# A windowed-attention and feed-forward kernel on one core: later exponentials kept as fp32 in PSUM, turns at PSUM banks in the work list, small key copies moved, list constants changed

## The chip, the cores and the metric

The kernel runs on one core of a Trainium2 chip. Its time is the device time of one execution in microseconds; lower is better. The core has TensorE (PE, matrix products), VectorE (DVE), ScalarE (ACT), GpSimd (POOL) and SyncE (SP), each with its own queue of instructions, which it works off in order; they wait for each other by semaphores. Sixteen DMA engines move data between HBM and the on-chip SBUF. Products land in PSUM, which has eight banks.

## The reference

Attention over 8 batches, 8 heads, 576 positions and head size 64, then a two-layer feed-forward part:

```
scores = q @ k^T / 8
heads 0-3: keep 0 <= i - j < 32
heads 4-7: keep 0 <= i - j < 128 and (i - j) % 4 == 0
attn = softmax over the kept scores;  x = attn @ v       (4608 x 512 after joining heads)
h = x @ w_in (512 x 2048);  g = max(0.01 h, h);  out = g @ w_out (2048 x 512)
```

All inputs and the output are fp32; the kernel works on fp16 operands.

## The kernel before, in words

**A list, planned and then issued.** The kernel first builds a list of tasks (`plan.add`). Each has the engines that may do it, an assumed duration for each, a delay until its result may be used, and the tasks it depends on. `_Plan.forward` plays the list through: it gives each task an engine and a start. `backward` turns that into priorities, and `run` repeats both nine times and keeps the best order. Then every engine's instructions are issued in the order of planned starts. So the order on every queue is fixed when the kernel is built, out of assumed durations; on the chip an instruction that finds its input late holds up everything behind it on its engine. `MARGIN` stretches the assumed durations after `CALM` microseconds; `LATE` and `RAMP` are additional delays assumed for the landing of loads. `FIRST` is the order of the loads of the first two batches and of the weights ("r" the last 64 positions of q and k, "q", "v" with batch and head group, "w" a 512 KB piece of the weights, "." a place for the second part of an earlier "v" load, "c" the mask tables).

`share` goes over the finished order and makes a cast of POOL wait for the VectorE task of kind "m" before it, where the two would run together.

**Attention.** One visit (`attend`, `turn`, `unit`) handles two heads of a batch, one on partitions 0-63 and one on 64-127. Queries and keys are loaded, cast to fp16 (`cast`, L387 on DVE and POOL, L386 on ACT), transposed and copied into slots (`move`, L400 on DVE and POOL, L398 on ACT). For the batches 0 and 1 TensorE transposes (L654, L697) into the PSUM bank `tp` (and, in batch 0, two more banks), and the copies read that bank. For the batches from 2 on VectorE transposes blocks of 32 (L619, L624, L631) in SBUF; in the dilated visits each half of the keys is then copied in two pieces, 64x512 and the last 64x64.

A visit has two units. In each, TensorE makes the scores of a narrow band of keys and queries into a bank `p_bank` (L775, tagged "s"), ScalarE takes the exponential (L782) and VectorE multiplies it with a table of zeros and ones (L786, tagged "m"). Batches 0 and 1 need no such mask, since TensorE adds a bias of -60000 there (`by_pe`, L771). A product with ones gives the sums, into the same `p_bank` (L793, or L810 where VectorE or POOL first added overlapping columns, L802), and a product with the values goes to a second bank (L793). ScalarE takes the logarithm (L818) of the sums and the exponential of its negative (L820), and VectorE multiplies this into the values' product (L831), which gives a piece of xt. The three banks sps, ops0 and ops1 go around for this (with hps and fps in the first batches); `ee` has four buffers for the exponentials.

**Feed-forward.** Twelve chunks of 384 rows. "Up" products of xt with w_in go to the banks hps (L850; L879 for the second chunk, in two halves), ScalarE applies the leaky activation into gt (L865, L891). "Down" products with w_out are plain for the first four 128-row tiles (L916, copied out at L924). The other tiles go in groups of four with seven half-size products in place of eight (L1006), for which VectorE forms sums of gt (L992) and of w_out (L946) and ScalarE and VectorE collect the results (L1035, L1037, L1043). The last three chunks do their "up" products in the same way (L1201, L1226, L1275, L1287, L1289, L1295, L1302). Attention of later batches and the feed-forward part of earlier ones run interleaved, so that between a unit's scores and its sums TensorE has other products to do.

The mask is these lines:

```
t_e = add("ACT", 0.06 + n * 0.00085, 0.22, [t_s] + e_old, ... activation(out=et, in_=p_bank, Exp))
t_m = t_e if by_pe else add("DVE", 0.45, 0.15, [t_e, t_con[0]],
        ... tensor_tensor(out=et, in0=et, in1=con[table], mult), prio, 0.0, "m")
```

## Time and profile before

| What | Value |
|---|---|
| Median of three runs | 298.88 us (297.12, 298.88, 300.25) |
| The profiled execution | 299.48 us, span 297.5 us |
| Granted TensorE clock | 1.0 |

The profile shows one execution. "Busy" is the time in which an engine had an instruction running. Matrix products are pipelined, so the rows of TensorE overlap, and a TensorE that is busy all the time is not thereby at its peak. Rows by line have the line, the engine, the operation, out<-in, the shapes and the count, then busy time in us, mean duration in ns, the engine's idle time before these instructions and what ended it. Rows in order of time start with the start and the duration in us; in brackets is the idle time before and what ended it.

### The profile page before, as it was taken

To read this page: it belongs to the slowest core of one execution; us is meant where nothing else is said; L and a number is where in the kernel's file an instruction comes from. 1 tells how busy PE (TensorE), PEld (TensorE's weight loads), DVE (VectorE), ACT (ScalarE), POOL (GpSimd) and SP (SyncE) were. 2 spreads that over 40 slices of the span, in tenths; PEclk is the share of its full clock that TensorE was granted. 3 is DMA by queue.
4 is the path that set the end of the run, shared out by engine and by line. 5 is a ranking of instruction groups with operands and counts; after the bars stand their busy time and mean duration, and the time that the engine had idled before them with its cause. 6 is when DMAs were issued, how large, how long until landed. Compare 5 with 4: busy or idle time off the path is not lost.

```text
span 297.5 us, 7792 instructions
## 1 busy us (share of the span) xinstructions
PE 284.5 (96%) x2975; PEld 225.4 (76%) x2975; DVE 218.1 (73%) x406; ACT 218.5 (73%) x502; POOL 144.0 (48%) x201
## 2 busy tenths in 40 slices
PE   5788989999999999999999999999999999999995
PEld 2665666678667788777777787776789999999984
DVE  6784375975689979738768869999757786587742
ACT  1797469678988884778878876886877787877611
POOL 5545555197778766776885759997100100000000
PEclk9999999999999999999999999999999999999999
DMA  7999999989988989988997998670101210111033
GB/s 216 325 303 402 322 356 249 140 165 169 155 181 175 210 187 149 231 164 173 205 150 197 166 211 160 145 211 3 36 16 53 79 36 2 37 71 39 35 108 106
DMA packets 155973, 47.16 MB, mean 159 GB/s; under 512 B 136736, under 2 KB 153248, under 8 KB 155936
## 3 DMA queue, kind: packets, MB, share of 16 engines
q1 hardware_dynamic: 155248, 46.04, 65.6%
q10 hardware_dynamic: 688, 0.63, 0.7%
q8 instruction: 23, 0.38, 0.6%
q14 instruction: 14, 0.11, 0.1%
HBM read 37.22 MB, written 9.44 MB: 157 GB/s over the span
## 4 chain that ended last, share of the span: by engine, by line
PE 75%; DMA 11%; DVE 5%; SPq 4%; issue 2%; ACT 1%; POOL 1%; DVEq 0%; POOLq 0%
PE hps L850 22%; PE fps L1006 21%; PE tp L1006 8%; PE hps L1275 5%; SPq L373 4%; DMA xt<-in_moe_w_out_dram 3%; PE ops L1275 3%; DMA vst<-in_v_dram 3%; DMA wst<-in_moe_w_in_dram 3%; PE ops L793 3%; PE fps L916 3%; PE hps L879 2%; PE ops L775 2%; DMA stg<-in_k_dram 2%; PE sps L793 1%
## 5 line engine op out<-in xcount | busy, mean ns | idle before, releaser
L850 PE MATMUL hps<-xt,w_in 128*128 128x384 f16 x488 | 95.2, 325 | 1.0 <-DVE w_in L387 0.6
L1006 PEld LDWEIGHTS <-gt 128*128 128x128 f16 x768 | 72.5, 98 | 9.8 <-DVE gt L992 0.4
L865 ACT ACTIVATE gt<-hps 128x384 f16<-128x384 f32 x122 | 59.1, 490 | 20.6 <-PE hps L850 19.5
L850 PEld LDWEIGHTS <-w_in 128*128 128x128 f16 x512 | 45.8, 98 | 23.9 <-issue 1.0
L387 POOL CAST slots<-vst 64x576 f16<-64x576 f32 (+2 forms) x60 | 52.2, 880 | 13.9 <-DVE ee L786 3.9
L387 POOL CAST nat<-stg 128x576 f16<-128x576 f32 (+1 forms) x55 | 41.4, 771 | 20.6 <-PE ops L793 6.8
L1006 PE MATMUL fps<-w_out,gt 128*128 128x256 f16 x368 | 47.0, 272 | 0.0
L786 DVE TENSOR_TENSOR ee<-ee,con 128x384 f16<-128x384 f16 (+1 forms) x48 | 22.2, 464 | 15.5 <-ACT ee L782 15.2
L820 ACT ACTIVATE rc<-rc 128x288 f32<-128x288 f32 x64 | 27.9, 442 | 0.9
L831 DVE TENSOR_TENSOR xt<-ops,rc 128x288 f16<-128x288 f32 x40 | 17.9, 448 | 11.9 <-ACT rc L820 7.7
L775 PEld LDWEIGHTS <-slots 128*128 128x128 f16 x320 | 18.4, 97 | 5.6 <-DVE slots L400 0.9
L400 POOL COPY slots<-turned 64x64 f16<-64x64 f16 (+2 forms) x36 | 19.2, 540 | 6.6 <-DVE turned L619 3.4
L793 PEld LDWEIGHTS <-slots 128*128 128x128 f16 x320 | 17.7, 97 | 4.9 <-issue 1.6
L1035 ACT COPY stg<-fps 128x512 f32<-128x512 f32 (+1 forms) x24 | 12.8, 531 | 11.1 <-PE fps L1006 10.4
L782 ACT ACTIVATE ee<-ops 128x384 f16<-128x384 f32 (+1 forms) x39 | 19.5, 503 | 1.7 <-PE ops L775 0.8
L398 ACT COPY slots<-turned 64x512 f16<-64x512 f16 (+1 forms) x28 | 18.6, 663 | 1.9 <-DVE turned L619 1.5
L818 ACT ACTIVATE rc<-ops 128x288 f32<-128x288 f32 x39 | 15.7, 408 | 5.7 <-PE ops L810 2.8
L802 POOL TENSOR_TENSOR ee<-ee 128x128 f16<-128x128 f16 x9 | 5.4, 601 | 29.2 <-DVE ee L786 29.2
L1302 ACT ACTIVATE gt<-slots 128x384 f16<-128x384 f32 x36 | 18.3, 526 | 0.9 <-DVE slots L1295 0.7
L619 DVE STREAM_TRANSPOSE turned<-nat 128x576 f16<-128x576 f16 x24 | 18.0, 761 | 0.1
L992 DVE TENSOR_TENSOR gt<-gt 128x1024 f16<-128x1024 f16 x21 | 17.1, 819 | 0.4 <-PE fps L1006 0.2
L1275 PEld LDWEIGHTS <-stg 128*128 128x128 f16 x192 | 16.3, 98 | 0.3
(137 smaller groups left out, 554.1 us busy)
## 6 DMA issues: line engine op xcount, KB each, us to landing
out_dram<-osb SPq DMA_DIRECT2D x32, 256.0 KB, 2.7
stg<-in_q_dram SPq DMA_DIRECT2D x48, 144.0 KB, 3.4
stg<-in_k_dram SPq DMA_DIRECT2D x48, 144.0 KB, 3.5
vst<-in_v_dram SPq DMA_DIRECT2D x14, 288.0 KB, 4.2
gt<-in_moe_w_in_dram SPq DMA_DIRECT2D x6, 512.0 KB, 7.1
vst<-in_v_dram SPq DMA_DIRECT2D x24, 128.0 KB, 3.0
stg<-in_q_dram SPq DMA_DIRECT2D x3, 512.0 KB, 9.7
stg<-in_k_dram SPq DMA_DIRECT2D x3, 512.0 KB, 9.5
```

The source lines that it names most:

```text
L387: return ENG[e].tensor_copy(out=dst, in_=src)
L398: nc.scalar.copy(out=dst, in_=src)
L400: ENG[e].tensor_copy(out=dst, in_=src)
L775: nc.tensor.matmul(p_bank[:, c:c + w], slot(tn, KB + 128 * s, 0, 128, [1, 128]), slot(tn, qx, 0, 128, *qd), start=first or not by_pe, stop ...
L782: lambda e: nc.scalar.activation(out=et[:, 0:n], in_=p_bank[:, 0:n], func=AF.Exp, scale=SCALE), prio)
L786: lambda e: nc.vector.tensor_tensor(out=et[:, 0:n], in0=et[:, 0:n], in1=con[:, table:table + n], op=ALU.mult), prio,
L793: nc.tensor.matmul(at(dst, 0, 128, o, *od), lhs(s), et[:, c:c + w], start=i == 0, stop=i == len(steps) - 1, skip_group_check=True)
L820: lambda e: nc.scalar.activation(out=rt, in_=rt, func=AF.Exp, scale=-1.0), prio)
L850: nc.tensor.matmul(ht[:, 0:n], at(w_in, 0, 128, vi * DFF + j // 2 * 256 + j % 2, [2, 128]), at(xt[m % 2], 0, 128, vi * 1152 + x0 + x, [1, n]),
L865: lambda e: nc.scalar.activation(out=gt[c % NG][:, j * n_c + x:j * n_c + x + n], in_=ht[:, 0:n], func=AF.Prelu, alpha=0.01),
L1006: nc.tensor.matmul(bk[:, x:x + HN], tl[:, off + j * step:off + j * step + 128], rhs(j), start=first and x == 0 and j == 0, stop=j == HJ - ...
L1275: nc.tensor.matmul(b[:, i * HT:i * HT + HT], lhs(v, j0 + i), rhs(v), start=first and i == 0 and v == 0, stop=i == 1 and v == 1, skip_group ...
```

## The change

It has four parts.

1. The exponentials of batches 2 to 7 are written as fp32 over the scores in `p_bank`, and the mask product reads them there and writes fp16 into `ee`. The wait for a free `ee` buffer moves from the exponential to the mask. The mask's assumed duration and its tag change ("m" becomes "M", so `share` no longer looks at it).
2. Copies out of the transposes' banks carry the bank's name, and `forward` lets such a copy start only when the one before it on that bank, if it was on another engine, is done.
3. The 64x64 key copy may go to POOL or ACT, not to POOL or DVE; some early casts may go to other engines than before.
4. Constants: delays, margins, the assumed cost of a VectorE cast, and the order of the first loads, where q00 now stands ahead of the second part of v01.

```
-ROOM, LATE = 256, 0.5
-RAMP = 0.0
+ROOM, LATE = 256, 1.5
+RAMP = 0.28
-MARGIN = {'ACT': 1.02, 'DVE': 1.062, 'POOL': 1.0, 'PE': 1.0, 'SP': 1.0, 'DMA': 1.133, 'LAND': 1.15}
-CALM = 38.8
+MARGIN = {'ACT': 1.036, 'DVE': 1.062, 'POOL': 1.0, 'PE': 1.006, 'SP': 1.0, 'DMA': 1.115, 'LAND': 1.15}
+CALM = 53.3
-FIRST = ('r0 q01 v01 . q00 w0 v00 . w1 w2 w3 w4 w5 w6 w7 w8 w9 w10 q11 w11 r1 v11 . w12 '
+FIRST = ('r0 q01 v01 q00 . w0 v00 . w1 w2 w3 w4 w5 w6 w7 w8 w9 w10 q11 w11 r1 v11 . w12 '
...
+        cached, bank_at = {}, {}
+
+        def when(t, eng):
+            who, done = bank_at.get(t.bank, (eng, 0.0))
+            return t.ready if who == eng or t.bank is None else max(t.ready, done)
...
-                        at = max(here, min(t.ready for t in could))
-                        pick = min(((t.ready + t.soft > at + 1e-9, t.prio, t.n), t)
-                                   for t in could if t.ready <= at + 1e-9)
+                        at = max(here, min(when(t, eng) for t in could))
+                        pick = min(((when(t, eng) + t.soft > at + 1e-9, t.prio, t.n), t)
+                                   for t in could if when(t, eng) <= at + 1e-9)
...
+            if t.bank is not None:
+                bank_at[t.bank] = (eng, t.done)
+                touched.update(("ACT", "DVE"))
...
-        cost = {"POOL": 0.15 + n * 0.00102 * slow, "DVE": 0.07 + n * (0.00055 if slow == 1.0 else 0.0011),
+        cost = {"POOL": 0.15 + n * 0.00102 * slow, "DVE": 0.07 + n * (0.00076 if slow == 1.0 else 0.0011),
...
-                             ("POOL", "DVE", "ACT") if first else ("POOL", "DVE"))
+                             (("DVE", "ACT") if g else ("POOL", "DVE", "ACT")) if first else ("POOL", "DVE"))
...
-                       at(st, 0, 64, o * 512 + 256 * g, [64, 2], [128, 2], [1, D]), 256, [lo] + r_old, prio)
+                       at(st, 0, 64, o * 512 + 256 * g, [64, 2], [128, 2], [1, D]), 256, [lo] + r_old, prio,
+                       ("POOL", "DVE") if b else ("DVE", "ACT"))
...
-                                    at(xk, p0, p1, 512, [1, D]), 64, [tk] + old, prio, ("POOL", "DVE")))
+                                    at(xk, p0, p1, 512, [1, D]), 64, [tk] + old, prio, ("POOL", "ACT")))
...
-                       512, after_q + old, prio, ("DVE", "ACT"), True)]
+                       512, after_q + old, prio, ("DVE", "ACT"), True, key(tpb))]
...
-        t_e = add("ACT", 0.06 + n * 0.00085, 0.22, [t_s] + e_old,
-                  lambda e: nc.scalar.activation(out=et[:, 0:n], in_=p_bank[:, 0:n], func=AF.Exp,
+        to = et if by_pe else p_bank
+        t_e = add("ACT", 0.06 + n * 0.00085, 0.22, [t_s] + (e_old if by_pe else []),
+                  lambda e: nc.scalar.activation(out=to[:, 0:n], in_=p_bank[:, 0:n], func=AF.Exp,
                                                  scale=SCALE), prio)
         t_m = t_e if by_pe else add(
-            "DVE", 0.45, 0.15, [t_e, t_con[0]],
-            lambda e: nc.vector.tensor_tensor(out=et[:, 0:n], in0=et[:, 0:n],
+            "DVE", 0.07 + n * 0.00118, 0.2, [t_e, t_con[0]] + e_old,
+            lambda e: nc.vector.tensor_tensor(out=et[:, 0:n], in0=p_bank[:, 0:n],
                                               in1=con[:, table:table + n], op=ALU.mult), prio,
-            0.0, "m")
+            0.0, "M")
```

The other copies out of transposes' banks get their bank's name in the same way.

More of the change, by code (lines that the diff above doesn't have):

```diff
@@ L54 @@
     __slots__ = ("choices", "eng", "lat", "deps", "fn", "prio", "soft", "n", "start", "done",
-                 "dur", "left", "ready", "users", "service", "kind", "late", "fixed", "rows", "yields")
+                 "dur", "left", "ready", "users", "service", "kind", "late", "fixed", "rows", "yields", "bank")
     def __init__(self, choices, lat, deps, fn, prio, soft, n, kind):
@@ L68, in __init__ @@
         self.yields = []
+        self.bank = None
 class _Plan:
@@ L129, in forward @@
                         if len(t.choices) > 1:
-                            end = max(here, t.ready) + dict(t.choices)[eng] * _margin(eng, here)
-                            if any(max(free.get(e, 0.0), t.ready) + d * _margin(e, here) < end - 0.02
+                            end = max(here, when(t, eng)) + dict(t.choices)[eng] * _margin(eng, here)
+                            if any(max(free.get(e, 0.0), when(t, e)) + d * _margin(e, here) < end - 0.02
                                    for e, d in t.choices if e != eng):
@@ L392, in clear, with move @@
                    lambda e: ENG[e].memset(dst, value), prio, 0.0, "set")
-    def move(dst, src, n, deps, prio, eng=("DVE",), dense=False):
+    def move(dst, src, n, deps, prio, eng=("DVE",), dense=False, bank=None):
         def fn(e):
@@ L402, in move @@
                 "POOL": 0.24 + n * 0.001}
-        return add(tuple((e, cost[e]) for e in eng), None, 0.2, deps, fn, prio)
+        t = add(tuple((e, cost[e]) for e in eng), None, 0.2, deps, fn, prio)
+        t.bank = bank
+        return t
     rings = {}
@@ L669, in turn @@
             mq = [move(slot(tn, 0, 0, 128, [144, 4], [1, 128]), at(tpb, 0, 128, 0, [128, 4], [1, 128]),
-                       512, after_q + old, prio, ("DVE", "ACT"), True)]
+                       512, after_q + old, prio, ("DVE", "ACT"), True, key(tpb))]
         else:
             mq = [move(slot(tn, 0, 0, 128, [4, 128], [1, 4]), at(tpb, 0, 128, 0, [1, 128], [128, 4]),
-                       512, after_q + old, prio, ("DVE", "ACT"))]
+                       512, after_q + old, prio, ("DVE", "ACT"), False, key(tpb))]
         mk = []
@@ L679, in turn @@
                                at(bk, p0, p1, c, [64, 2], [128, 4], [1, D]), 512, after_k + old, prio,
-                               ("DVE", "ACT"), True))
+                               ("DVE", "ACT"), True, key(bk)))
             else:
@@ L683, in turn @@
                                at(bk, p0, p1, c, [16, 8], [1, 16], [128, 4]), 512, after_k + old, prio,
-                               ("DVE", "ACT")))
+                               ("DVE", "ACT"), False, key(bk)))
         q_users += mq
@@ L690, in turn_rest @@
         c, r_users = raw[b, "rest"]
-        t_old, t_users = grab(hps[1] if b == 0 else tpb)
+        held = hps[1] if b == 0 else tpb
+        t_old, t_users = grab(held)
         bk = hps[1].bitcast(FP16) if b == 0 else tpb
@@ L710, in turn_rest @@
                 src = at(bk, 0, 128, g * 128, [64, 2], [1, D])
-            mq = move(dst, src, 128, [tts[1 - g]] + old, prio, ("DVE", "ACT"))
+            mq = move(dst, src, 128, [tts[1 - g]] + old, prio, ("DVE", "ACT"), False, key(held))
             mk = [move(slot(t0, KB + 1024 + 64 * hh, 64 * hh, 64 * hh + 64, [TS, 2], [1, D]),
                        at(bk, 64 * hh, 64 * hh + 64, 256 + g * 128, [64, 2], [1, D]), 128,
-                       [tts[1 - g]] + old, prio, ("DVE", "ACT")) for hh in range(2)]
+                       [tts[1 - g]] + old, prio, ("DVE", "ACT"), False, key(held)) for hh in range(2)]
             for vi in (2 * g, 2 * g + 1):
```

1 line of the change is left out of this document (removed).

## The prediction

> **What bounds the kernel now.** I read the first part of the page, then the busy time by stretches of ten microseconds, then TensorE's waits, and only then the groups that the change touches. The time given is that of one profiled execution: 299.48 us, of which 297.5 are the span. The three runs have a median of 298.88, 0.6 below it; the sum below is made against the profiled execution and moved down by 0.6 at its end.
>
> ```profile
> span 297.5 us, 7792 instructions
> PE 284.5 (96%) x2975; PEld 225.4 (76%) x2975; DVE 218.1 (73%) x406; ACT 218.5 (73%) x502; POOL 144.0 (48%) x201
> ```
>
> ```profile
> 0.00:20.00 20.00, 13.84 (x156) 8.76 (x157) 14.73 (x34) 12.00 (x27) 10.86 (x24) 1.00 0.91 276
> 30.00:40.00 10.00, 8.60 (x78) 5.95 (x76) 4.26 (x12) 4.79 (x10) 4.69 (x6) 1.00 1.10 329
> 80.00:90.00 10.00, 9.22 (x92) 6.36 (x91) 8.52 (x15) 9.04 (x23) 7.08 (x11) 1.00 0.87 179
> 90.00:100.00 10.00, 10.00 (x108) 7.59 (x107) 9.78 (x17) 8.04 (x20) 7.58 (x11) 1.00 0.96 198
> 190.00:200.00 10.00, 10.00 (x106) 7.49 (x104) 9.43 (x15) 9.04 (x22) 9.28 (x12) 1.00 0.62 170
> 200.00:210.00 10.00, 9.62 (x88) 7.05 (x86) 10.00 (x18) 7.31 (x18) 6.89 (x8) 1.00 0.16 55
> 290.00:298.00 8.00, 4.35 (x40) 3.65 (x38) 1.70 (x4) 1.49 (x4) 0.00 (x0) 0.98 0.28 98
> sum 298.00, PE 284.51 PEld 225.41 DVE 218.09 ACT 218.53 POOL 144.01; mean PE 9.81 PEld 7.77 DVE 7.52 ACT 7.54 POOL 4.97
> ```
>
> The columns are stretch, length, then busy time of PE, PEld, DVE, ACT, POOL, granted clock, DMA share. TensorE is idle 298.00 - 284.51 = 13.5 us. Of these, 20.00 - 13.84 = 6.2 lie in the first 20 us and 8.00 - 4.35 = 3.65 in the last stretch, behind the last matmul. Only 13.5 - 6.2 - 3.65 = 3.65 are left between 20 and 290 us: 1.40 in 30:40, 0.78 in 80:90, 0.38 in 200:210, the rest spread thinly. The change takes no matrix product away: built, it has 3 idle-filling 128x512 products in place of 5 and otherwise the same matmuls. So **what can be won in the middle is 3.65 us**, however much work leaves VectorE. Who holds TensorE up:
>
> ```profile
> PE hps L879 <- ACT gt L891: 1.4, 1, 1.4
> PE ops L793 <- ACT rc L818: 1.0, 2, 0.6
> ...
> PE ops L775 <- DVE xt L831: 0.3, 1, 0.3
> ```
>
> No row of that list names the mask (L786). TensorE's order is written out ahead, with other products between an exponential and its sum.
>
> **The change, part by part.**
>
> *The mask.* 48 exponentials (batches 2 to 7) now write fp32 over their scores in PSUM, and VectorE multiplies that with the fp16 table into ee. Before, both operands lay in SBUF.
>
> ```profile
> L786 DVE TENSOR_TENSOR ee<-ee,con 128x384 f16<-128x384 f16 x24 | 11.4, 479 | 9.0 <-ACT ee L782 8.8
> L786 DVE TENSOR_TENSOR ee<-ee,con 128x416 f16<-128x416 f16 x24 | 10.8, 449 | 6.5 <-ACT ee L782 6.4
> ```
>
> ```profile
> 200.53 0.91 DVE L786 TENSOR_TENSOR ee<-ee,con 128x416 f16<-128x416 f16 x1
> ...
> 205.83 0.36 DVE L786 TENSOR_TENSOR ee<-ee,con 128x416 f16<-128x416 f16 x1
> ```
>
> ```profile
> L831 DVE TENSOR_TENSOR xt<-ops,rc x40: 412/456/460, 13.3 to 238.6; 128x288 f16<-128x288 f32 x40
> ```
>
> ```profile
> L1295 DVE TENSOR_TENSOR slots<-hps,slots 128x384 f32<-128x384 f32 x16 | 8.9, 554 | 5.0 <-PE hps L1275 4.1 <-ACT slots L1287 0.6
> L1043 DVE TENSOR_TENSOR osb<-tp,stg 128x512 f32<-128x512 f32 x14 | 9.6, 686 | 4.2 <-PE tp L1006 2.5 <-ACT stg L1035 1.5
> ```
>
> One shape took 0.91 us and, five microseconds later, 0.36. The products with one operand in PSUM hold still: L831 spans 412 to 460 over all its places. From L1295 and L1043 a column costs (686 - 554)/128 = 1.03 ns, so the new mask takes 554 at 384 columns and 554 + 32 x 1.03 = 587 at 416. Sum: 24 x 0.554 + 24 x 0.587 = 27.4 us for 22.2, **+5.2 us of VectorE**, steady in place of scattered. Bounds per mask: it cannot fall under L831's 412, and 686 is the wider L1043. It lies beside TensorE's work, so I price it at nothing there while VectorE has room; the 0.2 us that a quiet mask (0.36) loses lengthens the chain from scores to sum, for which the waits show no price yet.
>
> The Trainium skill, VectorE: DVE Perf Modes, "The perf-mode tier table", speaks against this edit: a tensor_tensor of 16-bit SBUF operands runs at 2x and with any PSUM operand at 1x. The quiet rows (0.36 against 0.55) agree. By that rule alone each of the 48 masks loses 0.2 us, 9.6 us together; by the rows with their disturbed half, 5.2. The second rival below is this rule's outcome.
>
> *The exponential's destination.* No row shows ScalarE writing PSUM.
>
> ```profile
> L782 ACT ACTIVATE ee<-ops 128x416 f16<-128x416 f32 x19 | 9.8, 517 | 1.2 <-DVE gt L992 0.5 <-PE ops L775 0.4
> L782 ACT ACTIVATE ee<-ops 128x384 f16<-128x384 f32 x20 | 9.7, 491 | 0.4 <-PE ops L775 0.4
> L820 ACT ACTIVATE rc<-rc 128x288 f32<-128x288 f32 x64 | 27.9, 442 | 0.9
> L818 ACT ACTIVATE rc<-ops 128x288 f32<-128x288 f32 x39 | 15.7, 408 | 5.7 <-PE ops L810 2.8 <-PE ops L793 2.7
> ```
>
> A column costs (517 - 491)/32 = 0.81 ns. Worst: reading and writing one bank take turns, a second pass of 384 x 0.81 = 0.31 us, 48 x 0.31 = +15 us of ScalarE. Best: the destination saves what PSUM saves as a source, 442 - 408 = 34 ns, 48 x 0.034 = -1.6 us. I take zero, near the second, since the L818 rows show no penalty for PSUM. The score bank is held to L818 in either kernel, so no bank is lost.
>
> *Small key copies.* Built, the 64x64 copies go from 8 on DVE and 16 on POOL to none on DVE, 11 on POOL, 13 on ACT; ACT also gets 3 more of 64x576.
>
> ```profile
> L400 POOL COPY slots<-turned 64x64 f16<-64x64 f16 x16 | 4.9, 308 | 2.0 <-DVE turned L619 1.4
> L400 DVE COPY slots<-turned 64x64 f16<-64x64 f16 x8 | 2.6, 324 | 0.2
> L398 ACT COPY slots<-turned 64x576 f16<-64x576 f16 x11 | 7.3, 665 | 0.4 <-DVE turned L619 0.3
> ```
>
> ```profile
> L398 ACT COPY slots<-hps x4: 258/259/265, 8.0 to 10.1; 64x128 f16<-64x128 f16 x3, 128x128 f16<-128x128 f16 x1
> ```
>
> VectorE loses 2.6 us, leaving it 5.2 - 2.6 = +2.6. ScalarE gains at most 13 x 0.259 + 3 x 0.665 = 5.4 us, over the stretch below:
>
> ```profile
> 60.00:210.00 150.00, 148.83 (x1505) 113.70 (x1504) 121.85 (x209) 120.07 (x274) 113.34 (x150) 1.00 0.85 170
> ```
>
> There ScalarE is idle 150 - 120.07 = 29.9 us and VectorE 28.1. Both additions fit; I price them at nothing, and their cover is gone only where a stretch is already full, as 200:210 (DVE 10.00).
>
> *POOL's waits.* The old masks were of the kind that list code makes POOL's casts wait for; the new kind "M" is not. Built, 43 of 170 POOL copies wait for VectorE in place of 56 of 181. POOL is not on TensorE's list, so nothing directly; what it collides with next stands under the rivals.
>
> *Turns at PSUM banks and new constants.* Planned delays, margins and bank turns only reorder. The order of weight loads stays; ahead of them, q00 and its keys pass the tail of v01. Built, the values' products of the first four units stand behind the third and fourth units' scores, where the later tail lands. The one long stall:
>
> ```profile
> 31.88 1.03 PE L916 MATMUL fps<-w_out,gt 128*128 128x512 f16 x4
> ...
> 34.22 0.43 DVE L387 CAST nat<-stg 128x512 f16<-128x512 f32 x1 [0.87 <-DMA stg<-in_k_dram]
> ...
> 36.70 0.43 DVE L387 CAST w_out<-gt 128x512 f16<-128x512 f32 x1 [1.24 <-DMA gt<-in_moe_w_out_dram]
> ...
> 37.49 0.58 ACT L398 COPY slots<-tp 128x512 f16<-128x512 f16 x1 [1.82 <-DVE slots L400]
> ...
> 38.56 0.77 DVE L387 CAST w_out<-gt 128x512 f16<-128x512 f32 x1
> 38.90 0.82 PE L879 MATMUL hps<-xt,w_in 128*128 128x192 f16 x8 [1.41 <-ACT gt L891]
> ```
>
> ```profile
> 52.87 0.87 PE fps L916 x4
> ...
> 62.31 1.32 PE hps L879 x16
> ...
> 71.55 0.66 PE hps L850 x4
> ```
>
> VectorE sat behind a weight cast waiting for its DMA; the copies from bank tp behind it made ScalarE wait 1.82, and the activation that frees a bank came 1.41 late. Built, those three copies stand together on VectorE ahead of that cast, so the 1.41 goes. What is late next: TensorE now has only 4 products (0.66) between the L916 group's end, 31.88 + 0.87 = 32.75, and both transposes, whose key cast ends at 34.22 + 0.43 = 34.65. The first transpose is an estimated 0.22 (512 columns at the L850 row's 0.66/4/384 us): 34.65 - 32.75 - 0.66 - 0.22 = 1.0 idle. Then 4 L850, 24 L879 and 4 L916 products, 0.66 + 1.98 + 0.87 = 3.5 us, stand before an L916 group that needs the cast ending at 38.56 + 0.77 = 39.33: 4.7 - 3.5 = 1.2 idle. That is 2.2 in place of the 1.4 of 30:40, with some 0.6 of the work placed earlier or later, so a net of 0 to +0.4: I take **+0.2**. Elsewhere in the first 50 us I take 0, range -1.0 (a sixth of the 6.2 idle) to +1.0.
>
> *The late stalls.* 0.78 + 0.38 = 1.16 us in 80:90 and 200:210. In the second, VectorE is full and a 0.91 mask is in it; a steady 0.587 gives back 0.32. In the first, ScalarE's L818 was late behind the mask chain; the built order puts more products in between. I take **-1.0** of the 1.16, range 0 to -1.16.
>
> Sum: +0.2 - 1.0 = -0.8. 299.48 - 0.8 = 298.7, and less 0.6 for the median **298.1 us**.
>
> **The rivals.** *All idle time goes:* the steady mask and better order take the whole 3.65 (and nothing is lost early): 298.88 - 3.65 = 295.2. For it: the masks' means of 479 and 449 ns against the quiet 360 say that many are disturbed, and these get steadier. Against it: 1.4 of it is gated by landings that the change leaves where they are.
>
> *VectorE becomes the bound* (slower). Without its waits, POOL's casts fall on the two-SBUF-operand additions instead:
>
> ```profile
> L992 DVE TENSOR_TENSOR gt<-gt,gt x11: 676/686/1199, 88.3 to 281.7; 128x1024 f16<-128x1024 f16 x11
> ```
>
> L992 goes from 0.69 to 1.20, +0.5 each. In a full stretch three quiet masks (+0.2 each) and two such additions make +1.6 on a VectorE at 9.4 to 10.0: 1.0 to 1.6 over. With three stretches so full (90:100, 190:200, 200:210) that is about 4 us: 298.9 + 4 = 303. It decides once a full stretch gains over 0.6. Against it: over 60:210 VectorE has 28.1 us free, and 2.6 us of copies leave it.
>
> The Trainium skill, SBUF — State Buffer, "Who interferes with whom", has VectorE contend with GpSimd when both its inputs lie in SBUF and not with one there. The spread of L786 and the stillness of L831 agree; no run here yet shows the collisions that would move.
>
> *The exponential pays for PSUM twice:* +15 us on a ScalarE with 29.9 idle, but 9.04 full in 80:90 and 190:200; three exponentials add 0.9 there, next to nothing elsewhere; with the longer chain some +3 to 4: 302.5.
>
> **How the numbers follow.** About 1%, 3 us, is what a measurement here can tell from no change. My forecast (no change, 298.1; its own range 296.5 to 299.8) has 0.60; all idle gone 0.20, most of it beyond 1%; VectorE bound 0.13; the exponential twice 0.07. Faster by over 1%: 0.18; within: 0.66; slower: 0.16. The range reaches to the first rival's 295.2 and into the two slower ones: 295.0 to 301.5.
>
> **What would show it.** L786 at 0.55 and 0.59 with little spread, and not 0.36 to 0.91: the mask's price. L782 into ops near 0.49 and 0.52: the zero; near 0.8: the third rival. No 1.4 wait on L891, and two waits of about 1 us at the key transposes and the second L916 group in 33 to 40. DVE above 9.5 in more stretches, with PE waiting on L831 or L992: the second rival. The prediction is wrong if idle time between 20 and 290 us falls below 1.5 or rises above 6 us.

## The result, and the profile after

The changed kernel took 301.54 us (median of 20 runs, 299.53 to 303.35), the kernel before, beside it, 298.72 (20 runs, 297.11 to 301.41). The ratio is 1.0083, with a 95% interval of 1.0057 to 1.0108: **slower by 0.8%**. A second set of 12 runs (c0 below) gave 299.96 against 299.28, a ratio of 1.0033 (1.0003 to 1.0064). The ratios are estimated from the single runs, leave out those in a slower state of the chip (five of the 35 of the kernel before in the second set), and are not the quotients of the medians. So the loss is somewhere between 0.3 and 0.8%, 1 to 2.5 us.

The profiled execution of the changed kernel took 300.77 us. Its first lines, with the span and the busy time of each engine:

```profile
span 299.0 us, 7811 instructions
...
PE 285.6 (96%) x2973; PEld 226.6 (76%) x2973; DVE 219.1 (73%) x395; ACT 222.7 (75%) x520; POOL 137.8 (46%) x194
```

VectorE has 1.0 us more than before, ScalarE 4.2 more, POOL 6.2 less. The line numbers are some ten higher than before: the mask is L799 (before: L786), the exponential L795 (L782), the normalisation L844 (L831), the sums' additions of whole operands L1005 (L992), the product of the sums L823 (L810), the addition of overlapping columns ahead of it L815 (L802).

The stretches of the changed kernel (stretch, length, busy time of PE, PEld, DVE, ACT, POOL, granted clock, DMA share, GB/s):

```profile
20.00:290.00 270.00, 265.40 (x2775) 212.45 (x2775) 203.49 (x360) 208.61 (x486) 128.12 (x174) 1.00 0.66 152
30.00:40.00 10.00, 10.00 (x85) 6.71 (x84) 5.92 (x15) 5.69 (x15) 5.51 (x9) 1.00 1.08 355
50.00:60.00 10.00, 9.07 (x94) 5.33 (x92) 8.81 (x14) 5.74 (x15) 2.97 (x4) 1.00 0.96 159
70.00:80.00 10.00, 9.61 (x101) 6.62 (x98) 6.92 (x14) 9.64 (x23) 7.99 (x12) 1.00 1.01 176
80.00:90.00 10.00, 9.34 (x98) 6.80 (x95) 8.31 (x15) 9.45 (x24) 6.66 (x9) 1.00 0.93 182
110.00:120.00 10.00, 9.31 (x105) 8.34 (x103) 9.28 (x17) 4.75 (x11) 7.16 (x8) 1.00 0.85 151
200.00:210.00 10.00, 9.24 (x87) 6.90 (x85) 10.00 (x14) 7.33 (x16) 6.85 (x8) 1.00 0.08 29
```

The stop of 30:40 is gone in this execution (1.40 us idle before, 0.00 now); in the second profile of the same kernel, c0, that stretch has 0.66. New idle time stands in 50:60 (0.93), 70:80 (0.39), 110:120 (0.69) and 200:210 (0.76 in place of 0.38). TensorE's waits name them (engine and line, releaser: total, times, longest):

```profile
PE ops L823 <- POOL ee L815: 1.5, 2, 0.8
PE fps L665 <- DVE nat L395: 1.2, 1, 1.2
PE hps L863 <- ACT gt L878: 1.1, 2, 0.8
PE fps L929 <- DVE w_out L395: 0.8, 1, 0.8
```

The second stands at the start, near 7 us. None of the four was on the list of before in this size. The costliest is the addition of overlapping columns, which POOL now does 13 times in place of 9. The changed kernel near 202 us, first POOL and then TensorE:

```profile
198.62 3.45 POOL L395 CAST slots<-vst 64x576 f16<-64x576 f32 x3
202.15 0.69 POOL L815 TENSOR_TENSOR ee<-ee 128x128 f16<-128x128 f16 x1
```

```profile
201.90 0.23 PE L823 MATMUL ops<-ee,con 128*128 128x160 f16 x1
202.90 0.22 PE L823 MATMUL ops<-ee,con 128*128 128x128 f16 x1 [0.76 <-POOL ee L815]
```

POOL works off three casts, 3.45 us, and reaches the addition at 202.15; TensorE stands at the product that needs it. The masks and exponentials themselves:

```profile
L799 DVE TENSOR_TENSOR ee<-ops,con 128x416 f16<-128x416 f32 x16 | 9.2, 574 | 1.5 <-ACT ops L795 1.3
L799 DVE TENSOR_TENSOR ee<-ops,con 128x384 f16<-128x384 f32 x16 | 8.7, 549 | 7.3 <-ACT ops L795 7.3
...
L799 DVE TENSOR_TENSOR ee<-sps,con 128x416 f16<-128x416 f32 x8 | 4.6, 579 | 0.3 <-ACT sps L795 0.3
L799 DVE TENSOR_TENSOR ee<-sps,con 128x384 f16<-128x384 f32 x8 | 4.3, 543 | 0.8 <-ACT sps L795 0.7
```

```profile
L795 ACT ACTIVATE ops<-ops 128x416 f32<-128x416 f32 x16 | 8.1, 507 | 2.0 <-PE ops L787 1.9
L795 ACT ACTIVATE ops<-ops 128x384 f32<-128x384 f32 x16 | 7.6, 480 | 1.4 <-PE ops L787 1.4
```

Together the masks take 26.8 us in place of 22.2, and no TensorE wait names them.

**Where the loss lies.** Profiles of one and the same order begin to differ in the first 50 us, so two of them can't be set side by side from the start. One event divides them well: the landing of the last block of w_out, for which POOL's cast waits. From the kernel before, then the changed one:

```profile
51.19 0.87 POOL L387 CAST w_out<-xt 128x512 f16<-128x512 f32 x1 [1.16 <-DMA xt<-in_moe_w_out_dram]
```

```profile
50.85 0.87 POOL L395 CAST w_out<-xt 128x512 f16<-128x512 f32 x1 [1.14 <-DMA xt<-in_moe_w_out_dram]
```

Before: span 297.5 - 51.19 = 246.3 us from that landing to the end. After: 299.0 - 50.85 = 248.1. The opening took the changed kernel 0.3 us less, **the rest 1.8 us more**. How much of the time behind the landing TensorE was busy (the columns are those of the stretches above), again before and then after:

```profile
51.19:297.50 246.31, 241.90 (x2510) 196.03 (x2507) 186.48 (x333) 184.16 (x421) 116.93 (x155) 1.00 0.60 126
```

```profile
50.85:299.00 248.15, 241.69 (x2505) 196.19 (x2504) 186.08 (x322) 187.10 (x433) 112.20 (x152) 1.00 0.60 126
```

The busy time is the same to 0.2 us; the 1.8 us are idle time, 4.4 us before and 6.5 after. The table has these readings for every profiled execution of this study that loads the block:

| order | execution | landing, us | span, us | landing to end, us | TensorE idle in it, us |
|---|---|---|---|---|---|
| of before | kernel before | 51.19 | 297.5 | 246.3 | 4.4 |
| of before | e2, masks in PSUM | 50.48 | 296.8 | 246.3 | 4.4 |
| of before | b1, more warm-up | 51.68 | 298.2 | 246.5 | 4.6 |
| of before | e10, masks in PSUM, no waits for them | 49.60 | 296.0 | 246.4 | 4.6 |
| changed | changed kernel | 50.85 | 299.0 | 248.1 | 6.5 |
| changed | c0, the same again | 50.88 | 298.7 | 247.8 | 5.8 |
| changed | e4, more warm-up | 51.71 | 299.4 | 247.7 | 5.9 |
| changed, repaired | e3, sums | 49.84 | 297.0 | 247.2 | 4.7 |
| changed, repaired | e5, copies | 49.13 | 297.3 | 248.2 | 5.7 |
| changed, repaired | e8, sums and copies | 51.45 | 299.8 | 248.3 | 6.1 |
| changed, repaired | e7, sums, copies, warm-up | 49.37 | 295.9 | 246.5 | 4.6 |
| changed, repaired | e9, e7 and one more | 51.44 | 298.9 | 247.5 | 5.6 |
| planned anew | e1 | 50.25 | 301.0 | 250.8 | 7.9 |
| planned anew | p1 | 51.75 | 302.5 | 250.8 | 6.8 |
| planned anew | p2 | 50.02 | 299.7 | 249.7 | 7.5 |
| planned anew | r1 | 53.79 | 305.7 | 251.9 | 7.4 |
| planned anew | r2 | 50.24 | 299.2 | 249.0 | 5.3 |

The order of before gives 246.3 to 246.5 in four executions, whatever stands in the masks' operands; the changed order 247.7 to 248.1 in three. In all seven TensorE is busy 241.7 to 242.1 us behind the landing, so the difference of 1.2 to 1.8 us is idle time. In the orders planned anew that is not so: they have 242.2 to 244.5 us of busy time there, so part of what they lose is work that the opening left over or, in r1, products at half rate (last section). The landings of both orders, repairs included, scatter over the same 49 to 52 us.

### The profile page after: what moved, and what is told of

It is laid out like the page before. It is cut to its first block, busy times and chain, and to the rows that moved or that the text cites. A ratio compares the mean times of both kernels' runs of the same rounds, so it can differ in the third digit from the quotient of the medians.

```text
span 299.0 us, 7811 instructions
## 1 busy us (share of the span) xinstructions
PE 285.6 (96%) x2973; PEld 226.6 (76%) x2973; DVE 219.1 (73%) x395; ACT 222.7 (75%) x520; POOL 137.8 (46%) x194
## 4 chain that ended last, share of the span: by engine, by line
PE 65%; DMA 11%; POOL 7%; DVE 5%; ACT 5%; issue 3%; SPq 2%; POOLq 0%; DVEq 0%
PE fps L1019 17%; PE hps L863 17%; PE tp L1019 7%; DMA vst<-in_v_dram 5%; PE hps L1288 5%; POOL slots L395 3%; PE ops L1288 3%; DMA stg<-in_k_dram 3%; DMA wst<-in_moe_w_out_dram 3%; ACT gt L878 3%; PE fps L929 2%; PE ops L806 2%; SPq L381 2%; PE hps L892 2%; POOL nat L395 2%
## 5 line engine op out<-in xcount | busy, mean ns | idle before, releaser
L878 ACT ACTIVATE gt<-hps 128x384 f16<-128x384 f32 x122 | 58.7, 489 | 15.9 <-PE hps L863 14.6
L395 POOL CAST slots<-vst 64x576 f16<-64x576 f32 (+2 forms) x59 | 53.1, 905 | 15.6 <-DMA vst<-in_v_dram 13.1
L395 POOL CAST nat<-stg 128x576 f16<-128x576 f32 (+1 forms) x53 | 38.1, 738 | 30.6 <-DMA stg<-in_k_dram 15.7
L844 DVE TENSOR_TENSOR xt<-ops,rc 128x288 f16<-128x288 f32 x40 | 18.0, 449 | 14.0 <-ACT rc L833 10.8
L799 DVE TENSOR_TENSOR ee<-ops,con 128x384 f16<-128x384 f32 (+1 forms) x32 | 17.9, 561 | 8.8 <-ACT ops L795 8.7
L406 ACT COPY slots<-turned 64x512 f16<-64x512 f16 (+2 forms) x43 | 22.6, 533 | 1.0 <-DVE turned L630 0.3
L787 PEld LDWEIGHTS <-slots 128*128 128x128 f16 x320 | 18.8, 98 | 4.1 <-issue 0.4
L806 PEld LDWEIGHTS <-slots 128*128 128x128 f16 x320 | 18.3, 97 | 3.4 <-issue 0.7
L831 ACT ACTIVATE rc<-ops 128x288 f32<-128x288 f32 x39 | 15.9, 408 | 6.0 <-PE ops L806 3.5
L815 POOL TENSOR_TENSOR ee<-ee 128x128 f16<-128x128 f16 x13 | 7.8, 597 | 27.0 <-DVE ee L799 26.7
L795 ACT ACTIVATE ops<-ops 128x384 f32<-128x384 f32 (+1 forms) x32 | 15.7, 493 | 3.4 <-PE ops L787 3.3
L408 POOL COPY slots<-turned 64x64 f16<-64x64 f16 (+2 forms) x29 | 14.3, 497 | 8.1 <-DVE turned L630 3.3
L929 PE MATMUL fps<-w_out,gt 128*128 128x512 f16 x64 | 15.9, 378 | 0.9 <-DVE w_out L395 0.8
L1019 PE MATMUL fps<-wst,gt 128*128 128x256 f16 x128 | 16.4, 272 | 0.0
```

The lines of the kernel that those rows point to most:

```text
L395: return ENG[e].tensor_copy(out=dst, in_=src)
L406: nc.scalar.copy(out=dst, in_=src)
L787: nc.tensor.matmul(p_bank[:, c:c + w], slot(tn, KB + 128 * s, 0, 128, [1, 128]), slot(tn, qx, 0, 128, *qd), start=first or not by_pe, stop ...
L806: nc.tensor.matmul(at(dst, 0, 128, o, *od), lhs(s), et[:, c:c + w], start=i == 0, stop=i == len(steps) - 1, skip_group_check=True)
L878: lambda e: nc.scalar.activation(out=gt[c % NG][:, j * n_c + x:j * n_c + x + n], in_=ht[:, 0:n], func=AF.Prelu, alpha=0.01),
L929: nc.tensor.matmul(ft, g[:, j * n_c + tt * 128:j * n_c + tt * 128 + 128], w_out[:, j * DM:j * DM + DM], start=(j == 0), stop=(j == NJ - 1))
```

## The experiments

Theory A: the parts of the change cost nothing by themselves; the loss lies in stops that the newly planned order has behind the landing of the last weights. Theory B: the masks out of PSUM lengthen the chain from scores to sums and cost the loss in any order. Where "the order is kept", the plan of the kernel named is made as ever and single steps of it are altered behind `plan.run()`, so that all other instructions stay where they are. Each kernel was run beside the kernel before on the same chip.

**e1: the changed kernel with the old numbers.** LATE 0.5, RAMP 0, ACT 1.02, PE 1.0, DMA 1.133, CALM 38.8, q00 behind the dot, cast price 0.00055; an order planned anew.

> The changed kernel with only the numbers of the list put back (planned delay, ramp, margins, calm, cast price, place of q00); mask from PSUM, bank turns, engine choices and small copies stay as changed. The whole order is planned anew. Theory A (the loss of 2.8 us lies in places of the new order, above all the two column sums that POOL starts late, 0.69 and 0.76 us of stated wait and about 2 us of lag): the new numbers made that order, so the time leaves 301.5 and can land anywhere from 298 to 303; the start, whose engine choices stay, keeps its late first products. Theory B (the mask out of PSUM lengthens the chain and costs the 3 us whatever the order): 301 to 302 again.

Measured: 303.56 us, ratio 1.0174 (1.0123 to 1.0224). That is above the range of either theory. The new numbers do not cause the loss; without them the new parts have a worse order (250.8 from the landing on).

**e2: the masks alone, order kept.** The kernel before with

```diff
-lambda e: nc.scalar.activation(out=et[:, 0:n], in_=p_bank[:, 0:n], func=AF.Exp,
+lambda e: nc.scalar.activation(out=(et if by_pe else p_bank)[:, 0:n], in_=p_bank[:, 0:n], func=AF.Exp,
-out=et[:, 0:n], in0=et[:, 0:n],
+out=et[:, 0:n], in0=p_bank[:, 0:n],
```

> The kernel before, its order kept to the instruction, only the operands changed: the 48 exponentials write fp32 over their scores in PSUM and the masks read them there. Theory A: the masks take 0.55 and 0.58 us in place of a mean of 0.48 and 0.45, VectorE some 5 us more, and the time is that of the kernel before within 0.5 us, 298.2 to 299.2. Theory B: the longer chain alone gives the loss, 301 to 302.

Measured: 298.78 us, ratio 1.0001 (0.9974 to 1.0028). Its two largest groups of masks, and its span and landing (its line numbers are one higher than before):

```profile
L787 DVE TENSOR_TENSOR ee<-ops,con 128x416 f16<-128x416 f32 x16 | 9.3, 578 | 4.7 <-ACT ops L782 4.5
L787 DVE TENSOR_TENSOR ee<-ops,con 128x384 f16<-128x384 f32 x16 | 8.8, 553 | 6.7 <-ACT ops L782 6.7
```

```profile
span 296.8 us, 7806 instructions
```

```profile
50.48 0.87 POOL L387 CAST w_out<-xt 128x512 f16<-128x512 f32 x1 [1.90 <-DMA xt<-in_moe_w_out_dram]
```

All 48 masks are as slow as in the changed kernel, and the time is that of before within 0.3%. Theory B falls.

**e3: the two late sums.** The changed kernel, order kept, with

```diff
+for t in order:
+    if t.eng == "POOL" and t.kind == "m" and (115 < t.start < 117 or 201 < t.start < 202):
+        t.eng = "DVE"
```

> The changed kernel, its order kept, only the two additions of overlapping columns (L815) that POOL starts late (planned near 116 and 202 us) go to VectorE at the same place of the order. Theory A: TensorE's waits on them (0.69 and 0.76) go, and the lag of 0.9 and 1.2 us behind them; VectorE is full near 202, so some of the second comes back: 299.4 to 300.5 in place of 301.5. Theory B: nothing, 301 to 302.

Measured: 300.18 us, ratio 1.0034 (1.0003 to 1.0066). L823's wait of 1.5 us for POOL's L815 is gone (0.2 for VectorE's is left). From the landing to the end 247.2 us pass in place of 247.7 to 248.1, and 4.7 of them are idle in place of 5.8 to 6.5, which is near the 4.4 to 4.6 of the old order. In time it can't be told from the second set of the changed kernel (1.0033).

**e4: three more warm-up products.** The changed kernel, order kept, three products of 512 columns put behind the eight at the start.

> The changed kernel, its order kept, three more warm-up products of 512 columns behind the eight at the start, so that TensorE is busy until about 7.9 us, when the first real transpose starts, and not idle for 1.24 us. Theory A, its part at the start: products from 8 to 11.4 us run at full rate (512 columns in 0.22 and not 0.43 us) and the first units come 0.3 to 1.0 us sooner: 300.5 to 301.2. If the half rate there costs nothing because copies and landings set the pace: 301.5.

Measured: 299.94 us, ratio 1.0050 (1.0023 to 1.0078). The products run at full rate earlier (last section), but the landing came at 51.71 and the rest took 247.7: nothing lasting.

**c0: the changed kernel again.**

> The changed kernel once more, unchanged, beside the others of this set: 301 to 302, and a second profile of it. Earlier profiles of the same opening order began the first real product at 6.58 us and at 7.89 us, so the start is expected to differ from profile to profile by about 1.3 us whatever the kernel; the stops at the last weights (near 50 us), behind the key copies on ScalarE (70 to 80) and at the two late column sums (116 and 202) are expected again.

Measured: 299.96 us, ratio 1.0033 (1.0003 to 1.0064). That is below the range, so the ranges that start from 301.5 in the other runs lie too high. Its first real product began at 7.23, not at 7.89 (or the 6.56 of e3). TensorE is busy 9.61 of 70:80 and 9.22 of 200:210 as in the first profile, but 10.00 of 110:120: the stop at 116 is not in every execution.

**e5: two key copies off ScalarE.** The changed kernel, order kept, two 64x576 copies from ScalarE to VectorE (`if t.n in (576, 581): t.eng = "DVE"`).

> The changed kernel, its order kept, only the two 64x576 key copies (L406, 0.66 and 0.67 us) that ScalarE does at 72 and 75.5 us go to VectorE, which is busy 6.6 of 10 there. If they are why TensorE's next group waits on L878 near 77 us: the 0.65 us of lag gained between 70 and 90 us goes, 300.7 to 301.1. If ScalarE has room there, as the prediction held: 301.5 as the control.

Measured: 299.99 us, ratio 1.0056 (1.0025 to 1.0087). The stretch that they stood in, from e5:

```profile
70.00:80.00 10.00, 9.98 (x102) 6.88 (x101) 7.79 (x15) 8.92 (x23) 8.00 (x12) 1.00 1.05 196
110.00:120.00 10.00, 9.31 (x102) 7.97 (x100) 9.25 (x16) 4.20 (x10) 7.79 (x11) 1.00 1.02 191
```

TensorE is 9.98 busy in 70:80 in place of 9.61, so these copies caused most of that stop. At the end nothing of it is left: 110:120 has its stop again (c0 had none), landing to end takes 248.2, and in time it can't be told from c0.

**e6: the last weights not loaded.** The changed kernel, order kept; the load of the last 128x1024 of w_out is replaced by zeros set by POOL, so its result lacks that part.

> The changed kernel, its order kept, without the load of the last sixteenth of both weight matrices: zeros are set in its place, so that part of w_out is left out of the result. If the 1.2 to 1.9 us that the new order gains near 38 us are given back because TensorE then stands before the landing of these weights at 50 us: the wait of L929 on w_out (0.77 us) goes, and 300 to 301 remain of 301.5. If the stop at 50 us only takes the place of a later one: 301.5.

Measured: 299.47 us, ratio 1.0025 (0.9996 to 1.0053), against 1.0033 for c0: no difference that can be told. Theory A's part at this place missed. L929 still waits 0.65 us: POOL casts the zeros in its turn, at 49.95, behind a cast for which it waited 2.50 us on the landing of the block before. So the wait does not hang on the last piece alone; what else paces the opening was not taken apart further.

**e7: three repairs.** e3, e4 and e5 together.

> The changed kernel, its order kept, with three repairs together: the two late column sums on VectorE, the two key copies on VectorE, three more warm-up products. The sum of the single repairs: -1.4 (sums, from 301.5 to 300.2), -0.6 (copies, by the lag), -0.3 to -1.6 (warm-up): 298 to 299.3, level with the kernel before. If the loss lies elsewhere (the mask, the longer chains): 300.5 or more.

Measured: 298.82 us, ratio 0.9987 (0.9954 to 1.0019): level with the kernel before. Its span and landing:

```profile
span 295.9 us, 7811 instructions
```

```profile
49.37 0.87 POOL L395 CAST w_out<-xt 128x512 f16<-128x512 f32 x1 [0.94 <-DMA xt<-in_moe_w_out_dram]
```

**e8: the repairs without the warm-up.** e3 and e5 together.

> The changed kernel, its order kept, the two late column sums and the two key copies on VectorE, no more warm-up products. By the lags behind 70 us (the changed kernel loses 1.1 to 1.8 us there against before, the three repairs together 0.3): 298.5 to 299.3, and from the landing of the last weights to the end 246.6 us. If the warm-up products carried the gain of the three: 300.

Measured: 300.47 us, ratio 1.0050 (1.0019 to 1.0081), 248.3 from the landing on, 6.1 of it idle: missed. L823 waited 1.1 us in all for L815, now on VectorE. e7 and e8 differ in three products at the start, which bring nothing alone (e4, b1); their intervals just meet, so e7's level time can't be called the repairs' work.

**e9: a fourth repair.** e7, with one sum on VectorE (near 85 us) moved behind the L1005 that the next products need, those products moved ahead of the sum's product, and POOL's wait for that sum dropped.

> The three repairs and a fourth: near 85 us VectorE does the next products' operand (L1005) before the column sum, TensorE those products before the sum's, and POOL no longer waits for that sum. If the sum, 0.79 us beside POOL's casts, is what held the operand: the stop of 0.9 us near 85 goes, and from the landing of the last weights to the end it takes 245.7 to 246.2 us against 246.3 before; 297.6 to 298.5. If the late sum then delays its logarithm and the next scores as much: 246.6 again.

Measured: 300.05 us, ratio 1.0033 (1.0002 to 1.0065), 247.5 from the landing on, worse than either outcome. VectorE in e7 and then in e9:

```profile
83.64 0.91 DVE L1005 TENSOR_TENSOR rest<-gt 128x1024 f16<-128x1024 f16 x1
84.47 0.79 DVE L815 TENSOR_TENSOR ee<-ee 128x128 f16<-128x128 f16 x1
85.18 0.68 DVE L1005 TENSOR_TENSOR gt<-gt,gt 128x1024 f16<-128x1024 f16 x1
```

```profile
85.94 0.91 DVE L1005 TENSOR_TENSOR rest<-gt 128x1024 f16<-128x1024 f16 x1
86.88 1.15 DVE L1005 TENSOR_TENSOR gt<-gt,gt 128x1024 f16<-128x1024 f16 x1
87.95 0.79 DVE L815 TENSOR_TENSOR ee<-ee 128x128 f16<-128x128 f16 x1
```

Beside both stand three casts on POOL, from 83.22 on in e7 and from 85.53 on in e9. The operand comes first, as meant, but takes 1.15 us in place of 0.68, and TensorE waits 0.75 us for it; the sum takes 0.79 behind it as ahead of it, where the one before it in e7 took 0.22. The stop was not removed but handed on.

**b1: the kernel before with three more warm-up products,** order kept.

> The kernel before, its order kept, with three more warm-up products, so that TensorE is busy until the first landing. If the cold start costs time that lasts: 297.5 to 298.3 in place of 298.8. If the landing of the last weights near 50 us sets the opening whatever the start, as the profiles so far say (from that landing to the end the kernel before and the one with only its masks moved both take 246.3 us, the changed kernel 247.8 to 248.2): no change, 298.5 to 299.3.

Measured: 299.02 us, ratio 0.9997 (0.9963 to 1.0030); 246.5 from the landing on: no change. The first products do not set the time.

**p1: bank turns, first casts and key copies alone,** with the old masks and the old numbers; planned anew.

> The kernel before with the bank turns, the engine choices of the first casts and the small key copies of the change, but masks and numbers as before; the order is planned anew. The changed kernel with the old numbers took 303.6 to 303.9. If an order planned anew with numbers that were not chosen for it is what costs: slower than before here too, 300 to 303, in other places. If moving the masks is what makes the order bad: 298 to 299.5.

Measured: 303.85 us, ratio 1.0168 (1.0111 to 1.0225), above both ranges.

**p2: the masks alone, planned anew** with their new price and the old numbers.

> The kernel before with only the masks moved to PSUM, with their new price, and the order planned anew with the old numbers. With the order kept the same masks cost nothing (298.78 against 298.67). If the new order is what costs: 300 to 304. If the masks and the order are both harmless: 298 to 299.5.

Measured: 301.94 us, ratio 1.0082 (1.0045 to 1.0119), where the same masks in the old order (e2) gave 1.0001.

**r1: no part of the change, one planner number in its third decimal.** The kernel before with

```diff
-'DVE': 1.062
+'DVE': 1.06
```

> The kernel before with one planner number changed in its third decimal (VectorE's margin 1.062 to 1.060): the same work, the same operands, only an order planned anew. If any order that the numbers were not chosen for costs 1 to 4 us, as the changed kernel's does: 300 to 302. If orders are alike and the change's parts matter: 298.5 to 299.3.

Measured: 305.64 us, ratio 1.0220 (1.0176 to 1.0264). The tasks and their operands are those of before, on engines and in an order planned anew, and it loses 6.6 us, over twice the loss of the change and more than was expected. Its span, its landing and TensorE's longest waits:

```profile
span 305.7 us, 7785 instructions
```

```profile
53.79 0.87 POOL L387 CAST w_out<-xt 128x512 f16<-128x512 f32 x1 [1.39 <-DMA xt<-in_moe_w_out_dram]
```

```profile
PE hps L850 <- DVE w_in L387: 1.8, 3, 1.3
PE ops L810 <- POOL ee L802: 1.6, 2, 1.1
PE sps L810 <- POOL ee L802: 0.9, 2, 0.5
```

The late sum on POOL (L802, the changed kernel's L815) is here too, 2.5 us of it, without any mask in PSUM. But the late landing, 53.79, and a stretch of half granted clock behind a stop (last section) belong to this execution's loss as well. Of its six runs, the two with a mean granted clock of 1.0 took 304.35 and 305.08.

**r2: another planner number,** CALM 38.8 to 38.6.

> The kernel before with another planner number changed a little (the time from which margins count, 38.8 to 38.6 us): an order planned anew, all else the same. If any unchosen order costs: 300 to 306. If the first try was a bad draw: 298.5 to 299.5.

Measured: 301.66 us, ratio 1.0095 (1.0062 to 1.0128). r1 was not one bad draw: five orders planned anew gave +0.82, +0.95, +1.68, +1.74 and +2.20%. Behind r2's landing 5.3 us are idle and 243.7 busy, against 4.4 and 241.9 in the kernel before: its loss there is more work left over by the opening than stops.

**e10: masks in PSUM and POOL's waits for them dropped,** in the order of before (e2, with the kind "M").

> The kernel before, its order kept, masks in PSUM, and the waits of POOL's casts for masks dropped as in the change. If the masks, with one operand in PSUM, do not collide with POOL: 298.4 to 299.2, masks still at 0.55 and 0.58 with little spread. If POOL's casts then fall on VectorE's other additions: 299.5 to 301, L992 above its mean of before.

Measured: 298.71 us, ratio 0.9998 (0.9969 to 1.0027). Masks from 534 to 593 ns; the waits were worth nothing either way.

## Why the prediction was wrong, point by point

*What bounds the kernel.* Right: TensorE sets the time, and idle time between 20 and 290 us went from 270 - 266.32 = 3.68 (the row of before stands below) to 270 - 265.40 = 4.60. But one execution was read as the rule: three others of the old order have 2.6 to 3.2 us there, without the stop of 1.40 in 30:40, and c0 and e4 of the changed order 4.7 and 6.0. (The 3.65 us put behind the last product are 3.15, since the span ends at 297.5 and not at 298; the 3.65 in the middle stand.)

*The mask.* Right in size and in its price on the path: 549 and 574 ns forecast as 554 and 587, 26.8 us against 27.4, and e2 shows no price on the path within 0.3%. They hold still, 511 to 592 ns over all 48, where the 48 with both operands in SBUF went from 321 to 939. The Trainium skill, VectorE: DVE Perf Modes, "The perf-mode tier table", gives the slower tier with an operand in PSUM, and the trace agrees: the median went from 374 ns to 557. The measured price is 4.6 us of VectorE, not the 9.6 of that rule alone, and e2 shows no effect of it on the time.

*The exponential's destination.* Right: 480 and 507 ns into PSUM against 491 and 517 into SBUF, 10 ns faster, so even the sign of the small end held. The Trainium skill, ScalarE: Activation LUTs, "Step-by-step: what each stage is for", holds PSUM to be the lower-latency destination of the two; these rows agree. The third rival is out.

*The small key copies.* Right in size: 13 of 64x64 at 238 ns and three more of 64x576 make 5.1 us on ScalarE, against 5.4 at most. Wrong in the cover: in 70:80 ScalarE was already nearly full in the kernel before, in a row that the prediction did not show:

```profile
20.00:290.00 270.00, 266.32 (x2782) 213.01 (x2782) 201.67 (x369) 205.04 (x472) 133.15 (x178) 1.00 0.66 151
...
70.00:80.00 10.00, 10.00 (x109) 7.09 (x108) 6.94 (x14) 9.06 (x24) 8.15 (x12) 1.00 0.99 174
```

Its 9.06 became 9.64; TensorE then waited for L878, and e5 shows 0.37 us of that stretch to be two copies' doing. An average of 29.9 free us over 150 was used where a single stretch had under 1.

*POOL's waits.* Right: nothing (e10).

*The stop at L891 and the first 50 us.* The stop went, as forecast, but it was no mark of the old order: e2, b1 and e10 have that order and no such stop. Of the two waits forecast in its place the second, 1.2 us, came in no profile. The first, 1.0 us at the key transposes, is missing in the first profile of the changed kernel but stands in others of its order, with 0.66 us in c0, 0.84 in e3 and 0.98 in e4. From e4:

```profile
34.22 0.40 PE L665 MATMUL tp<-con,nat 128*128 128x128 f16 x4 [0.98 <-DVE nat L395]
```

So the mechanism of the first wait was read rightly, and it comes and goes with the execution. TensorE in e2:

```profile
32.94 1.03 PE L917 MATMUL fps<-w_out,gt 128*128 128x512 f16 x4
...
37.53 1.03 PE L917 MATMUL fps<-w_out,gt 128*128 128x512 f16 x4
38.39 0.82 PE L880 MATMUL hps<-xt,w_in 128*128 128x192 f16 x8
```

The first of these groups began at 31.88 in the kernel before, 1.06 us earlier, and the last, L879 there, waited 1.41 and began at 38.90; e2 came later to the first and did not wait. In the changed order TensorE can wait for weights near 50 us instead: L929 stood 0.77 us there, and 0.57 to 1.35 in e4, e7, e8 and e9, but not in c0, e3 and e5. That the one wait takes the other's place is not shown. The landing times of both orders scatter alike.

*The late stalls,* **the step that failed.** The prediction put them at -1.0 of 1.16 us. Measured: landing to end went from 246.3 in the kernel before to between 247.7 and 248.1, +1.4 to +1.8, all of it idle time of TensorE. 80:90 kept 0.66 of its 0.78, 200:210 went from 0.38 to 0.76, and new stops came in 70:80 and 110:120. The step asked what the parts do at the old order's stops and let the planned times and margins "only reorder". A new order brings its own stops, and r1 and r2 show how much an order alone can cost: +2.20 and +0.95% with no part changed. 301.54 lies just above the range's 301.5; that the second set's 299.96 lies inside it is owed to the width of the range, not to the mechanism. With +1.6 in place of -1.0 the sum would have been 299.48 + 0.2 + 1.6 - 0.6 = 300.7, between the medians of the two sets. The first set's loss, 2.8 us by the medians, is larger than these 1.4 to 1.8, the second set's, 1.0 by the ratio, smaller; what makes that difference is not shown.

*The rivals.* All idle time gone: no. VectorE as the bound: its time came near (303 forecast) but not by its mechanism, since the 64 instructions of L1005 have a mean of 785 ns where those of L992 had 797, and TensorE's waits name POOL's L815, ScalarE and a landing; still, its sentence on POOL holds where a sum stands behind POOL's casts. The Trainium skill, SBUF — State Buffer, "Who interferes with whom", has a VectorE instruction with two SBUF inputs contend with GpSimd reading there: L815 on VectorE took 0.22 us in one place of e7 and 0.79 in the midst of POOL's casts, which agrees. A rival "the order planned anew is worse by itself" was missing. The runs point to it by exclusion: e2 and e10 leave the masks and POOL's waits no part in the loss, and r1 and r2 lose as much or more with no part changed. The other parts were not run in the old order, nor the old masks in the changed one.

Where the idle time behind the landing grew can be read by stretches, for the four executions of the old order and the three of the changed one:

| stretch, us | idle, old order, us | idle, changed order, us |
|---|---|---|
| landing to 60 | 0.0 to 0.3 | 0.6 to 0.8 |
| 60 to 120 | 0.6 to 0.8 | 1.0 to 1.7 |
| 120 to 200 | 0.0 | 0.1 to 0.2 |
| 200 to 290 | 0.4 (e10: 0.9) | 0.8 |
| 290 to end | 3.2 | 3.2 |

What stays open: why the stops of one order differ from execution to execution, and what each is worth in time. e3 and e7 brought the idle time behind the landing to 4.7 and 4.6 us, near that of the old order, but e8 and e9, with the same sums and copies moved, only to 6.1 and 5.6, and the single repairs' times can't be told apart. No version was faster than the kernel before beyond doubt.

## What to carry to other kernels

Where a list scheduler sets the order, an edit's own price and the price of the order that it triggers are two experiments: alter the operands with the order kept, and plan anew with nothing altered; here the first gave 1.0001 and the second 1.0095 and 1.022. When executions start differently, measure from an event that all share (here the last landing), which made 0.2 us visible where whole runs scatter by 4; and read the idle time behind it, since an opening can also leave work over (r2). And look for an engine's free time in the stretch where the added work lands, not in its average.

## What the runs showed of the hardware that was not expected

How long the first products run at half rate differs with gaps between them. Changed kernel, then e4 with its three more warm-up products:

```profile
7.89 0.61 PE L665 MATMUL fps<-con,nat 128*128 128x128 f16 x4 [1.24 <-DVE nat L395]
...
9.37 1.06 PE L1416 MATMUL hps<-warm 128*128 128x512 f16 x2
```

```profile
6.32 0.81 PE L1416 MATMUL hps<-warm 128*128 128x512 f16 x3
7.29 0.40 PE L665 MATMUL fps<-con,nat 128*128 128x128 f16 x4 [0.16 <-DVE nat L395]
```

After 1.24 us of idleness four transposes took 0.61 us and two products of 512 columns 1.06; in e4 four transposes took 0.40 and three products 0.81. The gap alone does not make the transposes slow: in e3 they followed the warm-up products without one, at 6.56 us, and took 0.61 too, but the next four, at 7.63, took 0.40. With a gap ahead of them (1.24 us in the changed kernel, 0.58 in c0) the slow rate lasted until 11.4 and 11.7 us. The granted clock in these rows says 1.00 all along. The Trainium skill, TensorE: Matmul & The Clock Gate, "Part 1: The HAM clock gate", has the array run at half rate until about 3.4 us of sustained work. The executions without a gap reach the full rate 3.3 (e4) to 4.6 us (e3) after the first product at 3.05, which agrees roughly. It cost nothing in the end (e4, b1).

A stop can bring the half rate back, and then the clock column shows it. In r1 TensorE stood 1.13 us for the late sum on POOL and 0.50 us for ScalarE near 91 us; from 92 to 95 us the granted clock was 0.51. The same eight products in r1 and in the kernel before:

```profile
93.47 1.87 PE L1006 MATMUL fps<-wst,gt 128*128 128x256 f16 x8
```

```profile
93.15 1.03 PE L1006 MATMUL fps<-wst,gt 128*128 128x256 f16 x8
```

b1 has a clock of 0.50 from 11 to 14 us, behind stops of 0.99 and 0.49, and p1 from 36 to 38, behind one of 2.24. So a stop can cost more than its own idle time.

The landing of the last weights, with the same queues and the same order, scattered from 49.60 to 51.68 us over four executions of the old order (51.19 without b1, whose opening had the half clock). That is nearly all of the difference between their spans (296.0 to 298.2), and about half of the 4.3 us over which the kernel's 20 runs scatter.
